# Pooled attention with a feed-forward block: the last 128 keys' scores on all 128 rows, transposes behind the feed-forward's unit, heads in alternation

## The chip, the cores and the metric

The kernel runs on one core of one Trainium2 chip. A time is device microseconds (us) of one execution; three executions of the kernel before took 892.95, 895.72 and 897.29 us, median 895.72.

The engines are named as in the profile: PE is TensorE's matrix multiplications, PEld its loading of the stationary operand, DVE is VectorE, ACT ScalarE, POOL GpSimd, SP SyncE, which issues nearly all DMAs here. PSUM is the accumulator memory, eight banks of 512 fp32 columns on 128 partitions.

## The reference

```python
# q, k, v: (4 batches, 8 heads, 1152 positions, 64) fp32
q_pool = q.reshape(B, H, S // 2, 2, D).mean(axis=3)           # 576 pooled queries
scores = scale * np.matmul(q_pool, k.transpose(0, 1, 3, 2))   # 576 x 1152 a head
scores = scores - np.max(scores, axis=-1, keepdims=True)
attn = np.exp(scores); attn = attn / (np.sum(attn, axis=-1, keepdims=True) + 1e-09)
x = np.matmul(attn, v)        # heads side by side: (4, 576, 512)
xn = (x - mean) / np.sqrt(var + 1e-06) * g_ln
out = x + np.maximum(xn @ w_ch1, 0.0) @ w_ch2                 # 512 -> 2048 -> 512
```

## The kernel before

**Precision.** Most products are made of fp16 halves: an fp32 operand is scaled by a power of two and split into `hi` (fp16 of it) and `lo` (fp16 of the rest), and a product is three matmuls, hi by hi, hi by lo and lo by hi. ACT writes `hi` from PSUM, DVE writes `lo` (`split_from`, L267).

**Steps.** The 16 pairs of heads (4 batches of 4 pairs, `p`) have 9 steps each (`j`), 144 in all (`i = 9p + j`). A step is 128 pooled queries of one head against all 1152 keys; step `j == 4` has the last 64 queries of both heads. Before the change `j` 0 to 3 are the first head's four full chunks and 5 to 8 the second head's. A step's chain is: scores on PE (`emit_s`, L320), row maximum on DVE (L350), exponential on ACT (L364), fp16 halves on ACT (L378) and on DVE or, in every third step, POOL (L387, L385), a DMA transpose issued by SP (L390), and four steps after the scores attention times values on PE (`emit_pv`, L433). The first batch (steps 0 to 35) takes another way: PE transposes the fp32 exponentials itself (L397) and L421 multiplies in fp32, while DVE, ACT and POOL also prepare the feed-forward's weights.

**Scores.** Head dimension is 64, so a score matmul contracts 64 rows. Keys and queries lie twice on the partitions, 0 to 63 and 64 to 127. Keys 0 to 511 are taken from the upper 64 rows and keys 512 to 1023 from the lower 64, in turns (`wide`, L332), so that two matmuls of 512 columns run side by side in two halves of the array. The last 128 keys (`kt[..., 512:640]`) follow as three matmuls on rows 0 to 63 alone. PSUM holds two score slots of three banks; step `i` issues the scores of step `i + 1`, which wait until the exponential of step `i - 1` has left its slot.

**Preparation.** Six pieces of the next pair are transposed on PE, one a step (`PREPS`, L304, `a_prep`, L897): `prep_k` 0 and 1 (a head's first 1024 keys, fp32, 128 rows), `prep_k` 2 (the last 128 keys of both heads), `prep_q` 0 to 2 (six transposes of 64 rows each).

**Feed-forward.** When a block of 128 output rows has all 8 heads (`evacuated`, L879) it is queued for its norm (DVE, POOL, four PE transposes at L532 two steps later). With two blocks normed, `units_of` queues "units": `l1`, 24 matmuls of 256 columns (L569), and `l2`, 12 of 512 (L600; two units a block and weight half). From step 36 on at most one unit is issued a step (`some_units`, L902), after the last step two. One batch has 32 units, 36 steps pass a batch. Units, transposes and norms share PSUM banks 6 and 7 (`bank`, L501), and their evacuations wait in `evacs` for `flush` in the next step.

**Order.** Each engine runs in the order in which the Python program issues. `step` (L924) sets it: the row maximum, the scores of `i + 1`, `flush`, exponential, halves, norm, then on PE attention times values (`a_piece`), preparation (`a_prep`), unit (`some_units`).

Of the kernel before, what the change touches and what calls it, by code (L numbers as in the profile page):

```python
# [24 lines left out]
def tile_pooled_attention_moe(  # L25
# [33 lines left out]
    NORM_AT = (3, 4, 5, 6, 7)  # L59
# [52 lines left out]
    def load(p, which, eng):  # L112
        b, hp = divmod(p, HP)
        h = 2 * hp
        src = k if which == "k" else v
        r = raw_p.tile([128, 2, C, D], FP32, tag=which + "r", name=which + "r")
        eng.dma_start(out=r, in_=src[b, h:h + 2].rearrange("h (p c) d -> p h c d", c=C))
        raws[p, which] = r
# [26 lines left out]
    def kt_of(p):  # L145
        st = state(p)
        if "kt" not in st:
            st["kt"] = tr_p.tile([128, 2, 2, 640], FP16, tag="kt", name="kt")
        return st["kt"]
# [20 lines left out]
    def bound(p, which, o=0, n=128, junk=None):  # L170
# [4 lines left out]
        else:  # L175
            src = raws[p, which][o:o + n].rearrange("p a b d -> p (a b d)")
            if junk is None:
                junk = kt_of(p)[o:o + n].rearrange("p a h n -> p (a h n)")[:, 0:S]
        m = "kqv".index(which)
# [5 lines left out]
    def all_max(src, n, then):  # L185
# [8 lines left out]
        def one():  # L194
# [82 lines left out]
    def prep_k(p, u):  # L277
# [8 lines left out]
        for h in range(2):  # L286
            nc.tensor.transpose(ps[0:64, 128 * h:128 * h + 128], kr[:, h, C - 1], ident)
        x = ps[0:64, 0:256].rearrange("p (h n) -> p h n", h=2)
        return split_from((p, "k", 2), x, s[0:64, 0:1], kt[0:64, 0, :, 512:640], kt[0:64, 1, :, 512:640])

    def prep_q(p, u):
# [4 lines left out]
        ps = bank()  # L296
        for m in range(6):
            nc.tensor.transpose(
                ps[:, 64 * m:64 * m + 64], qr[:, 6 * u + m], ident[o:o + 64, o:o + 64]
# [4 lines left out]
    PREPS = ((prep_k, 0), (prep_k, 2), (prep_q, 0), (prep_q, 1), (prep_k, 1), (prep_q, 2))  # L304
# [15 lines left out]
    def emit_s(i):  # L320
# [3 lines left out]
        if j == 4:  # L324
            parts = [(h, h * C * 64 + 512, 64, 64 * h) for h in range(2)]
        else:
            h = 0 if j < 4 else 1
            parts = [(h, h * C * 64 + 128 * (j if h == 0 else j - 5), 128, 0)]
# [3 lines left out]
        wide = ((64, 0, 512, 0), (0, 512, 512, 0))  # L332
        for here in (wide, ((0, 1024, 128, 512),)):
            for a, r, c0, n, k0 in [(a, *x) for a in range(3) for x in here]:
                ka, qa = ((0, 0), (1, 0), (0, 1))[a]
                for h, q0, w, o in parts:
                    nc.tensor.matmul(  # L337
                        out=sp[o:o + w, c0:c0 + n],
                        lhsT=qt[r:r + 64, qa, q0:q0 + w],
                        rhs=kt[r:r + 64, ka, h, k0:k0 + n],  # L340
                        start=(a == 0),
                        stop=(a == 2),
                    )
        steps[i] = {"s": sp[:, 0:S]}
# [60 lines left out]
    def emit_pv(i, ps=None):  # L405
# [9 lines left out]
        else:  # L415
            parts = [(0 if j < 4 else 1, 0, 128, ps[:, 0:65])]
# [40 lines left out]
    def evac_pv(i, ps):  # L457
# [10 lines left out]
        else:  # L468
# [4 lines left out]
            h = 0 if j < 4 else 1  # L473
            o, n, m = 0, 128, 1
            x = xb[b][:, j - 5 * h, 128 * hp + 64 * h:128 * hp + 64 * h + 64]
# [77 lines left out]
    def half_of(w, xn, xs, stores, free=()):  # L553
# [36 lines left out]
        def l2(t, f0):  # L590
            if t == 0 and f0 == 4:
                flush()
            if f0 == 0:
# [4 lines left out]
            for f in range(f0, f0 + 4):  # L598
                for ha, wa in ((0, 0), (0, 1), (1, 0)):
                    nc.tensor.matmul(  # L600
                        out=ps,
                        lhsT=hv[0][:, ha, f, t * 128:t * 128 + 128],
                        rhs=wsl[:, 8 * w + 4 + f // 2, wa, (f % 2) * DM:(f % 2) * DM + DM],
                        start=(f == 0 and ha == 0 and wa == 0),
# [472 lines left out]
```

## Time and profile before

| | |
|---|---|
| median of three executions | 895.72 us |
| profiled execution, its own time | 892.43 us |
| its span, first to last instruction | 890.6 us |
| PE busy | 837.2 us, 94% |
| DVE busy | 611.8 us, 69% |
| ACT busy | 568.4 us, 64% |
| POOL busy | 346.6 us, 39% |
| mean granted TensorE clock | 0.98 of full speed |

Busy time of an engine is the time in which at least one of its instructions runs; PE's matmuls overlap, so a group of n matmuls is busy for less than n times the mean duration of one. How often PE can start a matmul is read from the start times of two groups in the timeline. The granted clock has two levels, 1.2 and 2.4 GHz, and a share between stands for a stretch with both.

### The profile page before, as it was taken

The numbers are of one execution on the slowest core, as the hardware profiler recorded it, in microseconds if no ns is written. First come the engines' busy times: TensorE is split into PE (matmuls) and PEld (weight loads), VectorE is DVE, ScalarE is ACT, GpSimd is POOL, SyncE is SP. The second block draws the span as 40 slices with busy tenths as digits, with TensorE's granted clock in tenths as the row PEclk, the third lists the DMA queues.
The fourth block names the chain that finished last, engine by engine and source line by source line (L and its number), as shares of the span: only waits on it lengthen the run. The fifth ranks groups of instructions, "written<-read, shape, count | busy, mean of one in ns | idle before, by whom it ended". The sixth has DMA issues, their size and how long they took to land.

```text
span 890.6 us, 22107 instructions
## 1 busy us (share of the span) xinstructions
PE 837.2 (94%) x9430; PEld 608.2 (68%) x9430; DVE 611.8 (69%) x1094; ACT 568.4 (64%) x851; POOL 346.6 (39%) x316
## 2 busy tenths in 40 slices
PE   8898979899799999996999999998999999999997
PEld 6787768677566676754758576676667576776664
DVE  3586988888787777778777777787777777532211
ACT  4888788788677777776677777676767666211110
POOL 3010543543988844336435243535543422300000
PEclk9999999999899999997999999999999999999999
DMA  4554154403498779997896979895979778310001
GB/s 130 196 157 164 50 194 126 172 1 96 92 179 168 141 150 183 180 169 137 154 193 114 203 141 188 127 186 107 222 121 175 129 129 143 57 25 13 13 13 24
DMA packets 271667, 114.95 MB, mean 129 GB/s; under 512 B 254928, under 2 KB 254928, under 8 KB 271568
## 3 DMA queue, kind: packets, MB, share of 16 engines
q1 hardware_dynamic: 271216, 112.65, 61.4%
q8 instruction: 74, 1.21, 0.6%
q10 hardware_dynamic: 352, 0.88, 0.4%
q14 instruction: 25, 0.20, 0.1%
HBM read 45.09 MB, written 4.72 MB: 56 GB/s over the span
## 4 chain that ended last, share of the span: by engine, by line
PE 54%; DVE 25%; ACT 10%; DMA 5%; issue 3%; POOL 2%; SPq 1%; ACTq 0%; POOLq 0%; DVEq 0%
PE psum L569 15%; PE psum L600 15%; DVE mx L350 7%; PE psum L337 7%; PE psum L433 7%; DVE hl L387 4%; PE psum L421 4%; DVE stage L107 3%; ACT pe L364 3%; PE psum L397 2%; DVE ht L583 2%; DVE wsl L107 2%; DVE kt L270 2%; DMA qr<-in_q_dram 2%; DMA kr<-in_k_dram 1%
## 5 line engine op out<-in xcount | busy, mean ns | idle before, releaser
L350 DVE TENSOR_REDUCE mx<-psum 128x1 f32<-128x1152 f32 x144 | 194.2, 1349 | 27.1 <-PE psum L433 18.9
L364 ACT ACTIVATE pe<-psum,nb,sc 128x1152 f32<-128x1152 f32 x144 | 188.9, 1312 | 32.0 <-DVE nb L355 23.6
L600 PE MATMUL psum<-wsl,ht 128*128 128x512 f16 x864 | 196.0, 379 | 0.2 <-DVE ht L583 0.2
L569 PEld LDWEIGHTS <-wsl 128*128 128x128 f16 x1920 | 170.9, 98 | 22.7 <-issue 2.7
L569 PE MATMUL psum<-xn,wsl 128*128 128x256 f16 x1536 | 177.3, 274 | 1.9 <-DVE xn L539 1.0
L337 PE MATMUL psum<-kt,qt 64*128 64x512 f16 (+3 forms) x1440 | 151.8, 332 | 24.7 <-ACT xb L488 13.9
L337 PEld LDWEIGHTS <-qt 64*128 64x128 f16 (+1 forms) x1440 | 70.9, 98 | 116.0 <-issue 66.4
L600 PEld LDWEIGHTS <-ht 128*128 128x128 f16 x864 | 81.8, 98 | 90.0 <-issue 0.4
L378 ACT ACTIVATE hl<-pe 128x1152 f16<-128x1152 f32 x108 | 125.7, 1163 | 5.0 <-DMA pt<-hl 1.6
L433 PE MATMUL psum<-vt,pt 128*128 128x65 f16 (+1 forms) x3240 | 119.8, 195 | 0.0
L433 PEld LDWEIGHTS <-pt 128*128 128x128 f16 (+1 forms) x3240 | 108.1, 101 | 9.4 <-issue 0.6
L488 ACT ACTIVATE xb<-psum,r 128x64 f32<-128x64 f32 x128 | 39.7, 311 | 109.4 <-DVE r L484 100.1
L244 POOL TENSOR_SCALAR pe<-pe 128x1152 f32<-128x1152 f32 x36 | 41.9, 1164 | 164.0 <-ACT hl L378 153.7
L387 DVE SCALAR_TENSOR_TENSOR hl<-pe,hl 128x1152 f16<-128x1152 f32 x72 | 104.3, 1448 | 0.0
L582 ACT ACTIVATE ht<-psum 128x512 f16<-128x512 f32 x72 | 42.7, 594 | 90.6 <-PE psum L569 90.2
L583 DVE SCALAR_TENSOR_TENSOR ht<-psum,ht 128x512 f16<-128x512 f32 x72 | 49.6, 690 | 66.2 <-ACT ht L582 65.4
L385 POOL TENSOR_TENSOR hl<-pe,hl 128x1152 f16<-128x1152 f32 x36 | 86.4, 2400 | 3.0
L421 PE MATMUL psum<-pt,vt 128*65 128x128 f32 (+1 forms) x720 | 81.6, 271 | 0.0
L421 PEld LDWEIGHTS psum<-pt,vt 128*65 128x65 f32 x720 | 75.8, 144 | 0.2 <-issue 0.2
L270 DVE SCALAR_TENSOR_TENSOR qt<-psum,s,qt 128x384 f16<-128x384 f32 x48 | 29.6, 616 | 46.9 <-ACT qt L273 46.9
L270 DVE SCALAR_TENSOR_TENSOR kt<-psum,s,kt 128x512 f16<-128x512 f32 (+1 forms) x48 | 31.5, 658 | 39.1 <-ACT kt L273 39.1
L403 ACT COPY pt<-psum 128x512 f32<-128x512 f32 x72 | 44.9, 639 | 10.8 <-PE psum L397 5.5
(112 smaller groups left out, 925.6 us busy)
## 6 DMA issues: line engine op xcount, KB each, us to landing
stage<-in_moe_w_ch_dram SPq DMA_DIRECT2D x32, 512.0 KB, 5.5
kr<-in_k_dram SPq DMA_DIRECT2D x16, 576.0 KB, 4.7
qr<-in_q_dram SPq DMA_DIRECT2D x31, 288.0 KB, 6.2
vr<-in_v_dram SPq DMA_DIRECT2D x15, 576.0 KB, 4.9
out_dram<-xb SPq DMA_DIRECT2D x32, 128.0 KB, 2.4
pt<-hl SPq DMA_TRANSPOSE x108, 5.0
vr<-in_v_dram ACTq DMA_DIRECT2D x1, 576.0 KB, 6.5
out_dram<-xh SPq DMA_DIRECT2D x4, 128.0 KB, 3.5
```

Of the source, the lines that this page charges most:

```text
L270: nc.vector.scalar_tensor_tensor(lo, ps, s, hi, op0=ALU.mult, op1=ALU.subtract)
L337: nc.tensor.matmul(out=sp[o:o + w, c0:c0 + n], lhsT=qt[r:r + 64, qa, q0:q0 + w], rhs=kt[r:r + 64, ka, h, k0:k0 + n], start=(a == 0), stop= ...
L350: nc.vector.tensor_reduce(mx, st["s"], axis=AX.X, op=ALU.max)
L364: nc.scalar.activation(out=st["pe"], in_=st["s"], func=ACTF.Exp, scale=pair[i // C]["sc"][:, 0:1], bias=st["nb"],)
L378: nc.scalar.activation(out=hl[:, 0], in_=st["pe"], func=ACTF.Copy, scale=2.0 ** 15)
L385: nc.gpsimd.tensor_tensor(hl[:, 1], st["pe"], hl[:, 0], op=ALU.subtract)
L387: nc.vector.scalar_tensor_tensor(hl[:, 1], st["pe"], 2.0 ** 15, hl[:, 0], op0=ALU.mult, op1=ALU.subtract)
L421: nc.tensor.matmul(out=ps[0:65, q0:q0 + w], lhsT=vt[:, h, c], rhs=pt[:, 128 * u + q0:128 * u + q0 + w], start=(u == 0), stop=(u == C - 1),)
L433: nc.tensor.matmul(out=dst[:, 0:n], lhsT=lhsT, rhs=rhs, start=(u == 0 and lhsT is hi and n == 65), stop=(u == C - 1 and lhsT is lo), skip_ ...
L569: nc.tensor.matmul(out=ps[:, o:o + n], lhsT=wsl[:, 8 * w + cc, wa, f * 128:f * 128 + 128], rhs=xn[:, xa * KD + cc, 0:n], start=(m == 0), s ...
L583: lambda: nc.vector.scalar_tensor_tensor(lo, pv, 0.0, hi, op0=ALU.max, op1=ALU.subtract),
L600: nc.tensor.matmul(out=ps, lhsT=hv[0][:, ha, f, t * 128:t * 128 + 128], rhs=wsl[:, 8 * w + 4 + f // 2, wa, (f % 2) * DM:(f % 2) * DM + DM] ...
```

## The change

1. The last 128 keys of a head are stored as `k8`, `hi` on rows 0 to 63 and `lo` on rows 64 to 127 (`prep_k` 2 transposes the chunk beside a copy of itself, which a second, small DMA puts next to it). Two matmuls on all 128 rows, query `hi` and query `lo` against `k8`, take the place of three on 64 rows. The product lo by lo is thereby added.
2. `some_units` stands ahead of `a_prep` in a step, and in `PREPS` `prep_k` 1 stands ahead of `prep_q` 1.
3. In the last two pairs of each batch (`p % 4` of 2 and 3) the heads alternate (`PLACES`), so that an output block has all its heads earlier and the four blocks of a batch come further apart.
4. In the first batch's units the second block's `l2` is three units of 8 matmuls and not two of 12 (`fine`).
5. In `all_max` one small DVE operation reads PSUM (`max(ps, mx) * ident`) in place of SBUF.

```diff
+    PLACES = [[(h, t) for h in range(2) for t in range(4)], [(h, t) for t in range(4) for h in range(2)]]
+    for x in PLACES:
+        x.insert(C // 2, None)
...
+        x = src[b, h:h + 2].rearrange("h (p c) d -> p h c d", c=C)
+        if which == "k":
+            r = raw_p.tile([128, 2, C + 1, D], FP32, tag="kr", name="kr")
+            eng.dma_start(out=r[:, :, 0:C], in_=x)
+            eng.dma_start(out=r[:, :, C], in_=x[:, :, C - 1])
...
-                nc.vector.tensor_scalar(dg[0:n, 0:n], ident[0:n, 0:n], mx[0:n], None, op0=ALU.mult)
+                nc.vector.scalar_tensor_tensor(
+                    dg[0:n, 0:n], ps[0:n, 0:n], mx[0:n], ident[0:n, 0:n], op0=ALU.max, op1=ALU.mult
+                )
...
         for h in range(2):
-            nc.tensor.transpose(ps[0:64, 128 * h:128 * h + 128], kr[:, h, C - 1], ident)
-        x = ps[0:64, 0:256].rearrange("p (h n) -> p h n", h=2)
-        return split_from((p, "k", 2), x, s[0:64, 0:1], kt[0:64, 0, :, 512:640], kt[0:64, 1, :, 512:640])
+            x = kr[:, h, C - 1:C + 1].rearrange("p c d -> p (c d)")
+            nc.tensor.transpose(ps[:, 128 * h:128 * h + 128], x, ident)
+        x = ps[:, 0:256].rearrange("p (h n) -> p h n", h=2)
+        k8 = pair[p]["k8"]
+
+        def low():
+            nc.vector.scalar_tensor_tensor(
+                k8[64:128], x[64:128], s[64:128, 0:1], k8[64:128], op0=ALU.mult, op1=ALU.subtract
+            )
+            have.add((p, "k", 2))
+
+        return (lambda: nc.scalar.activation(out=k8, in_=x, func=ACTF.Copy, scale=s[:, 0:1]), low)
...
-    PREPS = ((prep_k, 0), (prep_k, 2), (prep_q, 0), (prep_q, 1), (prep_k, 1), (prep_q, 2))
+    PREPS = ((prep_k, 0), (prep_k, 2), (prep_q, 0), (prep_k, 1), (prep_q, 1), (prep_q, 2))
...
-            parts = [(h, h * C * 64 + 128 * (j if h == 0 else j - 5), 128, 0)]
+            parts = [(PLACES[p % HP // 2][j][0], 128 * j, 128, 0)]
...
+        for qa in range(2):
+            for h, q0, w, o in parts:
+                nc.tensor.matmul(
+                    out=sp[o:o + w, 1024:1152],
+                    lhsT=qt[:, qa, q0:q0 + w], rhs=pair[p]["k8"][:, h],
+                    start=(qa == 0), stop=(qa == 1),
+                )
...
-            (2 * w + 1, 2 + f0 // 2, lambda t=t, f0=f0: l2(t, f0))
-            for t in range(len(xs)) for f0 in (0, 4)
+            (2 * w + 1, (m1 + 5) // 6, lambda t=t, m0=m0, m1=m1: l2(t, m0, m1))
+            for t in range(len(xs))
+            for m0, m1 in (((0, 8), (8, 16), (16, 24)) if t and fine else ((0, 12), (12, 24)))
...
-            pre(i0 + (4, 5, 6, 6, 7, 8)[n] + late, lambda fn=fn, p=p, u=u: preps.append((fn, p, u)))
+            pre(i0 + 4 + n + late, lambda fn=fn, p=p, u=u: preps.append((fn, p, u)))
...
-        key = ("h", b // 2) if j == 4 else (b, j if j < 4 else j - 5)
+        key = ("h", b // 2) if j == 4 else (b, PLACES[p % HP // 2][j][1])
...
                 a_piece(i)
+            some_units(i)
             a_prep()
-            some_units(i)
```

What stands on PE around a step's query transposes, in a step of the second half. Before (`pt` is the transposed attention, `qr` the raw queries, `ht` the feed-forward's hidden layer):

```order
L433 LDWEIGHTS pt
L433 MATMUL psum<-vt,pt 128x65
L298 MATMUL psum<-ident,qr 128x64 x6
L600 LDWEIGHTS ht
L600 MATMUL psum<-wsl,ht 128x512
```

The unit stands between the transposes and the next scores. In the changed kernel, the same place to the end of the next scores (L632 is `l2`, L325 the transposes, L362 and L370 the scores, L464 attention times values; `qt` are the transposed queries):

```order
L632 MATMUL psum<-wsl,ht 128x512
L325 MATMUL psum<-ident,qr 128x64 x6
L362 LDWEIGHTS qt
L362 MATMUL psum<-kt,qt 128x512
...
L370 LDWEIGHTS qt
L370 MATMUL psum<-kt,qt 128x128
L370 LDWEIGHTS qt
L370 MATMUL psum<-kt,qt 128x128
L464 LDWEIGHTS pt
```

The transposes moved behind the unit and stand right before the scores, as they do in 28 of the 33 steps with query transposes from step 42 on (in the other five a norm's transposes stand between); before, a unit follows them in all 33. The last 128 keys are two matmuls; before they are three, with `L337` rows of the same look.

ACT around steps 74 to 76, where one batch's units have ended and the next batch's begin. Before (`pe` is the exponential, `hl` its half, `xb` an output block, `xn` a normed block, `ht` an `l1` unit's evacuation):

```order
L364 ACTIVATE pe<-psum,nb,sc 128x1152
L378 ACTIVATE hl<-pe 128x1152
L180 ACTIVATE kt,acc<-vr 128x1152
L488 ACTIVATE xb<-psum,r 128x64
L364 ACTIVATE pe<-psum,nb,sc 128x1152
L378 ACTIVATE hl<-pe 128x1152
L488 ACTIVATE xb<-psum,r 128x64
L538 CAST xn<-psum 128x4x128
L364 ACTIVATE pe<-psum,nb,sc 128x1152
L378 ACTIVATE hl<-pe 128x1152
L488 ACTIVATE xb<-psum,r 128x64
L273 ACTIVATE kt<-psum,s 128x512
```

The same stretch in the changed kernel:

```order
L395 ACTIVATE pe<-psum,nb,sc 128x1152
L409 ACTIVATE hl<-pe 128x1152
L191 ACTIVATE kt,acc<-vr 128x1152
L519 ACTIVATE xb<-psum,r 128x64
L395 ACTIVATE pe<-psum,nb,sc 128x1152
L409 ACTIVATE hl<-pe 128x1152
L519 ACTIVATE xb<-psum,r 128x64
L613 ACTIVATE ht<-psum 128x512
L395 ACTIVATE pe<-psum,nb,sc 128x1152
L409 ACTIVATE hl<-pe 128x1152
L519 ACTIVATE xb<-psum,r 128x64
L613 ACTIVATE ht<-psum 128x512
```

The rows run from the exponential of step 74 to the evacuations behind that of step 76. An `l1` unit's evacuation (`ht`) stands behind the exponentials of steps 75 and 76; before, the first one stands behind that of step 78. Counted over all steps from 36 on, PE has no unit in steps 36 to 40 and 73 to 77 in the kernel before, and in steps 36, 37 and 74 in the changed one; the first batch's units are 32 before and 36 now. On POOL, two norms stand between the first weight piece (L244 `wsl`) of step 36 and the low half (L385) of step 38 before, and one now.

## Rows read from the trace of the kernel before

**Rows 1.** Page, part 1: busy us, share, instructions of each engine.
```profile
PE 837.2 (94%) x9430; PEld 608.2 (68%) x9430; DVE 611.8 (69%) x1094; ACT 568.4 (64%) x851; POOL 346.6 (39%) x316
```

**Rows 2.** Windows: five stretches, busy us (instructions) of each engine, clock, DMA.
```profile
core 0: us, PE busy (x) PEld busy (x) DVE busy (x) ACT busy (x) POOL busy (x), PEclk, DMA share, GB/s
207.00:225.00 18.00, 15.11 (x130) 11.55 (x128) 15.91 (x34) 15.87 (x23) 9.35 (x17) 0.91 0.54 132
225.00:239.00 14.00, 9.75 (x104) 7.36 (x100) 11.76 (x21) 6.96 (x11) 13.47 (x13) 0.76 0.52 98
246.00:394.00 148.00, 145.31 (x1795) 99.31 (x1792) 112.16 (x201) 105.80 (x142) 92.05 (x65) 1.00 0.89 165
401.00:426.00 25.00, 17.46 (x215) 12.18 (x213) 20.48 (x45) 16.32 (x23) 18.12 (x26) 0.73 0.80 143
753.00:891.00 138.00, 132.88 (x1142) 92.78 (x1140) 40.11 (x72) 21.36 (x39) 7.97 (x17) 1.00 0.14 27
```

**Rows 3.** Timeline of stalls: start us, us, engine, work, [idle before <-releaser].
```profile
230.62 1.31 ACT L364 ACTIVATE pe<-psum,nb,sc 128x1152 f32<-128x1152 f32 x1 [5.00 <-POOL hl L385]
231.99 1.78 PE L337 MATMUL psum<-kt,qt 64*128 64x512 f16 x9 [3.67 <-ACT pe L364]
...
404.98 1.81 PE L337 MATMUL psum<-kt,qt 64*64 64x512 f16 x18 [2.82 <-ACT pe L364]
...
419.81 0.63 PE L287 MATMUL psum<-ident,kr 128*64 128x128 f32 x2 [3.92 <-DVE kt L270]
```

**Rows 4.** Matmul groups by shape: busy us, mean ns of one, idle before.
```profile
L337 PE MATMUL psum<-kt,qt 64*128 64x512 f16 x768 | 110.2, 385 | 6.3 <-ACT pe L364 3.7 <-ACT pt L403 2.1 <-DVE qt L270 0.3
L337 PE MATMUL psum<-kt,qt 64*128 64x128 f16 x384 | 42.6, 218 | 13.6 <-ACT xb L488 12.0 <-ACT xh L488 1.6
L569 PE MATMUL psum<-xh,wsl 128*128 128x128 f16 x384 | 22.6, 219 | 0.7 <-DVE xn L539 0.7
L337 PE MATMUL psum<-kt,qt 64*64 64x128 f16 x96 | 5.6, 222 | 2.0 <-ACT xb L488 1.9
```

**Rows 5.** Timeline of TensorE, query transposes ahead of a unit.
```profile
567.42 0.99 PE L433 MATMUL psum<-vt,pt 128*128 128x65 f16 x27
568.34 0.58 PE L298 MATMUL psum<-ident,qr 64*128 64x64 f32 x6
568.86 2.76 PE L600 MATMUL psum<-wsl,ht 128*128 128x512 f16 x12
571.55 0.99 PE L337 MATMUL psum<-kt,qt 64*128 64x512 f16 x9
572.47 1.90 PE L433 MATMUL psum<-vt,pt 128*64 128x65 f16 x54
```

**Rows 6.** Timeline of TensorE, a step with key transposes.
```profile
552.06 0.99 PE L433 MATMUL psum<-vt,pt 128*128 128x65 f16 x27
552.88 0.63 PE L284 MATMUL psum<-ident,kr 128*128 128x128 f32 x4
553.35 2.78 PE L569 MATMUL psum<-xn,wsl 128*128 128x256 f16 x24
```

**Rows 7.** Timeline of TensorE, query transposes ahead of scores, two places.
```profile
56.73 0.46 PE L298 MATMUL psum<-ident,qr 64*128 64x64 f32 x4
...
57.90 0.42 PE L700 MATMUL psum<-g,stage 128*128 128x1 bf16 x8
...
98.46 0.40 PE L298 MATMUL psum<-ident,qr 64*128 64x64 f32 x3
...
99.80 0.43 PE L700 MATMUL psum<-ones,stage 128*128 128x1 bf16 x8
```

**Rows 8.** Page, parts 5 and 6: L433 matmuls, key loads, DMA transposes.
```profile
L433 PE MATMUL psum<-vt,pt 128*128 128x65 f16 (+1 forms) x3240 | 119.8, 195 | 0.0
kr<-in_k_dram SPq DMA_DIRECT2D x16, 576.0 KB, 4.7
pt<-hl SPq DMA_TRANSPOSE x108, 5.0
```

More of the change, by code (lines that the diff above doesn't have):

```diff
@@ L115, in load @@
         src = k if which == "k" else v
-        r = raw_p.tile([128, 2, C, D], FP32, tag=which + "r", name=which + "r")
-        eng.dma_start(out=r, in_=src[b, h:h + 2].rearrange("h (p c) d -> p h c d", c=C))
+        x = src[b, h:h + 2].rearrange("h (p c) d -> p h c d", c=C)
[3 more added lines that the diff above has]
+            eng.dma_start(out=r[:, :, C], in_=x[:, :, C - 1])
+        else:
+            r = raw_p.tile([128, 2, C, D], FP32, tag="vr", name="vr")
+            eng.dma_start(out=r, in_=x)
         raws[p, which] = r
@@ L324, in emit_s @@
         if j == 4:
-            parts = [(h, h * C * 64 + 512, 64, 64 * h) for h in range(2)]
+            parts = [(h, 128 * j + 64 * h, 64, 64 * h) for h in range(2)]
         else:
-            h = 0 if j < 4 else 1
-            parts = [(h, h * C * 64 + 128 * (j if h == 0 else j - 5), 128, 0)]
+            parts = [(PLACES[p % HP // 2][j][0], 128 * j, 128, 0)]
         for h, q0, w, o in parts:
@@ L331, in emit_s @@
             assert need <= have, (i, need - have)
[L332 to L335, printed above, removed]
+        for a in range(3):
+            ka, qa = ((0, 0), (1, 0), (0, 1))[a]
+            for r, c0 in ((64, 0), (0, 512)):
                 for h, q0, w, o in parts:
                     nc.tensor.matmul(
[L338 to L342, printed above, removed]
-                    )
+                        out=sp[o:o + w, c0:c0 + 512],
+                        lhsT=qt[r:r + 64, qa, q0:q0 + w], rhs=kt[r:r + 64, ka, h],
+                        start=(a == 0), stop=(a == 2),
+                    )
+        for qa in range(2):
[5 more added lines that the diff above has]
+                )
         steps[i] = {"s": sp[:, 0:S]}
@@ L597, in l2 @@
             ps = acc[t]
[L598 to L604, printed above, removed]
-                        stop=(f == 7 and ha == 1),
-                    )
-            if f0 == 0:
+            for m in range(m0, m1):
+                f = m // 3
+                ha, wa = ((0, 0), (0, 1), (1, 0))[m % 3]
+                nc.tensor.matmul(
+                    out=ps,
+                    lhsT=hv[0][:, ha, f, t * 128:t * 128 + 128],
+                    rhs=wsl[:, 8 * w + 4 + f // 2, wa, (f % 2) * DM:(f % 2) * DM + DM],
+                    start=(m == 0), stop=(m == 23),
+                )
+            if m1 < 24:
                 return ()
@@ L827, in half @@
                 w, keep["xn", u], [xb[b][:, u], xb[b][:, u + 1]],
-                [[(64 * s, rows(b, 2 * x + s)) for s in range(2)] for x in (u, u + 1)],
+                [[(64 * s, rows(b, 2 * x + s)) for s in range(2)] for x in (u, u + 1)], b == 0,
             )
```

33 lines of the change are left out of this document (19 added, 14 removed).

## The prediction

> **What bounds the kernel now.** I read the page's busy times first: PE is busy for 837.2 of 890.6 us, DVE for 611.8 [rows 1]. An average hides stages, so the windows came next. In the long stretches of the second half PE is busy for 145.3 of 148 us at the full clock, and in the tail, where only feed-forward units are left, for 132.9 of 138, while DVE has 112.2 of 148 and 40 of 138 [rows 2]. There, what PE does sets the time: a microsecond less work on PE is a microsecond less. In two stretches it is not so. From 225 to 239 us, where the first batch's attention is done and its feed-forward has not begun, PE is busy for 9.75 of 14 us at a granted clock of 0.76; from 401 to 426, between the first batch's units and the second's, for 17.5 of 25 us at 0.73 [rows 2]. The timeline names the waits: PE stands 3.67 us for an exponential that itself stood 5.00 us for POOL, then 2.82 us for an exponential and 3.92 us for DVE's half of the keys [rows 3]. A clock of 0.76 means that part of the stretch ran at 1.2 GHz in place of 2.4; both low stretches begin with PE standing. Units are work without a deadline, so whatever PE loses here is not made up: the tail is as long as the units left over.
>
> So the change has two ways to gain, less PE work and fewer of these holes.
>
> **Narrow scores (the last 128 keys).** Three matmuls of 128 columns are busy for 42.6/128 = 0.333 us together, one lasts 0.218, so they start (0.333 - 0.218)/2 = 0.058 us apart [rows 4]. A matmul of 128 columns on all 128 rows costs 22.6/384 = 0.059 us in a stream [rows 4]. Three become two, so a step saves 0.058; 128 full steps give 7.4 us. The 16 steps of half chunks have three couples of 64-wide matmuls, busy 5.6/16 = 0.35 us [rows 4]; they become four matmuls, and I put them at nothing.
>
> The trace has no matmul on 128 rows behind one on 64 rows within the scores. It has the change between them elsewhere: from attention times values to query transposes (64 rows) takes 0.92 us, to key transposes (128 rows) 0.82 [rows 5, 6], so going from 128 to 64 rows costs 0.10. For the way back I take the same. A step's scores have one change at each end before and after; it moves from behind the narrow matmuls to ahead of them, at no cost. Bounds: if a second change is paid, the term is 128 x (0.058 - 0.10) = -5.4 us; if the change is hidden under the last wide matmul, 128 x (0.058 + 0.10) = +20. I take 7.4, the value of rows of the same shape.
>
> The Trainium skill ("TensorEngine Tiling (Array Packing)", Tiling Modes) says that changing the tiling mode drains the TensorE. The trace agrees that a change costs, but with 0.10 us. A wide matmul lasts 0.385 [rows 4] and the next starts 0.216 later (12 of 512 columns take 2.69 - 0.10 [rows 5]), so a full emptying behind it would cost 0.17. By that rule the term would be 7.4 - 128 x 0.07 = -1.6 us.
>
> The new product's preparation stays off PE's path: ACT and DVE take 256 columns as before, the transposes are as many. They hide behind PE's step of some 5 us (30 steps in the 148 us of the long window [rows 2]); DVE's spare time there is 36 of 148 us.
>
> **Query transposes behind the unit.** Before, a step with them goes from 567.42 to 572.47: attention times values with the change of rows 0.92, transposes with the change back 0.52, unit 2.69 with a change, scores 0.92 [rows 5]. In the changed order attention times values go to the unit without a change (0.82, [rows 6]), the unit to the transposes with one, and the transposes to the scores without. That last border is in the trace, in the first batch, where no units are: transposes and scores together take 57.90 - 56.73 = 1.17 us where the queries lie on the upper 64 partitions (odd pairs) and 99.80 - 98.46 = 1.34 on the lower (even pairs) [rows 7], against 0.52 + 0.92 = 1.44 apart. The first scores run beside the last transposes, in the other half of the array. With the 0.10 at the front, odd pairs save 0.37 a piece and even ones 0.20. Of the 33 steps concerned, 28 get the scores directly behind (11 odd, 17 even, counted in the order); five have a norm between and keep three changes. Sum: 11 x 0.37 + 17 x 0.20 = 7.5 us. Key transposes use 128 rows like the units on both sides, so their move is worth nothing.
>
> **The holes.** The order has no unit in five steps at each of the two places before, and in two and one now. At 401 to 426, full-speed work is at most 17.46 x 0.73 = 12.7 us, so 12.3 are lost [rows 2]; one step of five keeps a fifth, 9.8 come back. At 225 to 239, 14 - 9.75 x 0.76 = 6.6 are lost. The exponential's wait behind POOL has one norm less in its queue, and units are there three steps earlier; I let 1.1 remain and count 5.5. The loss of 18 - 15.11 x 0.91 = 4.3 at 207 to 225 lies in steps 36 to 38 and is kept. Bounds for both together: nothing, if the hole only moves, and 19 us, if it closes. The third batch's border shows no such hole and counts nothing. The split into units of 8 adds no matmul; it serves to fill four more steps and is priced in this term.
>
> **What is added.** Each pair's key load gets a second DMA of 64 KB, a ninth of a load that lands in 4.7 us [rows 8]; SP issues it behind that load and ahead of DMA transposes. Cost between 0.5 (a ninth) and 4.7 us a pair. Transposes land in 5.0 us and are read three steps, some 15 us, after their issue, and attention times values have an idle time of 0.0 [rows 8], so I cost it at nothing; without that cover it would be 0.5 to 4.7 us on each of 11 pairs. The small DVE operation in `all_max` is one for one.
>
> **Sum.** 7.4 + 7.5 + 9.8 + 5.5 = 30.2 us. The profiled execution took 892.43 us, which gives 862.2; the median of the runs is 3.3 above that execution, so I forecast 865.5, written as 865.
>
> **Rivals.**
> 1. *DVE or ACT becomes the bound in the refilled steps.* DVE is busy for 20.5 of 25 us and 11.8 of 14 in the two holes [rows 2], with the norms' work among it; units add evacuations there. Against it: the norms come further apart, and PE's lack of work made the steps stand on a chain, not on DVE's throughput. If half of the holes' 15.3 us stays, the time is 873.
> 2. *The narrow matmuls pay a change on both sides*, -5.4 in place of 7.4: 878. For it: nothing in the trace shows this border. Against it: one end of the scores loses its change. Milder, *the array empties behind the wide matmuls*, 0.17 in place of 0.10 a step, -1.6 in place of 7.4: 874; the borders in [rows 5, 6] speak against it. This is what the Trainium skill's rule above would give.
> 3. *The narrow border is hidden* under the wide matmuls, or waits for PSUM banks shrink too: up to 12 us better, 853.
> 4. *Slower: the DMA queue falls behind.* The DMA share is 0.89 over 148 us [rows 2], and a faster PE raises it to about 0.92. If the extra transfer costs a whole load (4.7 us) with no cover, each of 11 pairs makes PE stand for it: 52 us, 865 + 52 = 917. It decides once transposes land later than three steps after issue, that is 15 in place of 5 us [rows 8]; idle time of 0.0 there speaks against it. The Trainium skill ("DMA: Bandwidth & Descriptors", Specifications) asks for 512 B a transfer for full rate, and the new rows have 256; by that the small DMA runs slower than its size says, which no row here shows.
>
> **How the numbers follow.** Forecast (857 to 871) 0.60; rival 1, 0.15; rival 2, 0.06, and the emptying 0.03; rival 3, 0.08; rival 4, 0.03; and 0.05 for holes that stay as they are with a dear narrow border (7.5 - 5.4 = 2 us gained, 893). The range of 853 to 878 takes in rivals 1 to 3 up to their prices and leaves out the last two and the tails. About 0.5%, 4.5 us, is what a measurement of this kernel tells from no change: faster by more 0.92, within 0.05, slower 0.03.
>
> **What would show it.** Narrow scores: from the first score matmul to what follows 0.86 us in place of 0.92; 0.96 is rival 2. Query steps: transposes and scores together 1.1 to 1.3 us. Holes: no wait over 2 us on PE between 225 and 426, granted clock over 0.9 in both stretches, or else rival 1. DMA: L433's successor still without idle time. The tail behind the last step must be shorter by about what the holes gave. I am wrong if PE's busy time falls by less than 10 us, or if waits on DVE or ACT take over what it gives up.

## The result and the profile after

The changed kernel takes 883.98 us (median of 4 runs, 880.98 to 886.67), the kernel before beside it 896.5 (892.95 to 898.92): ratio 0.987, 95% interval 0.984 to 0.990. It is 12.5 us faster, where 30 were forecast; 884 lies outside the range of 853 to 878. The profiled execution of after took 883.46 us, with a span of 881.7.

The page's busy times answer to [rows 1], and four windows to [rows 2]; the last is shorter because the run is. Lines of after: units L600 and L632 (before L569, L600), scores L362 and, narrow, L370 (L337), attention times values L464 (L433), query transposes L325 (L298), `all_max` L207 (L196), ACT's bounds L191 (L180).

```profile
PE 823.7 (93%) x9270; PEld 587.6 (67%) x9270; DVE 614.7 (70%) x1092; ACT 570.7 (65%) x851; POOL 349.0 (40%) x318
```

```profile
225.00:239.00 14.00, 11.34 (x129) 8.56 (x127) 11.55 (x18) 7.20 (x9) 8.69 (x10) 0.88 0.42 80
246.00:394.00 148.00, 137.40 (x1699) 90.61 (x1700) 115.01 (x200) 103.90 (x137) 88.93 (x66) 0.98 0.86 161
401.00:426.00 25.00, 21.68 (x288) 15.62 (x283) 21.05 (x42) 19.06 (x26) 10.87 (x16) 1.00 0.86 156
753.00:882.00 129.00, 124.01 (x1063) 85.09 (x1061) 35.95 (x65) 19.99 (x36) 7.83 (x15) 0.99 0.14 29
```

PE's work fell by 13.5 us, the time by less. The two holes did fill: work at full speed rose from 12.7 to 21.7 us at 401 to 426 and from 7.4 to 10.0 at 225 to 239 (busy by clock), 11.6 of the 15.3 forecast. Behind the last attention times values the run lasts 110.0 us in place of 118.5. But the steps up to there end when they did, at 771.7 us (before: 772.1): what is gained is the feed-forward units that they took in, and nothing shows of less work in the steps themselves. The stretch between the holes, where PE had been busy for 145.3 of 148 us at the full clock, now stands for 10.6 us at 0.98.

PE's waits in the steps from 240 to 755 us, first before, then after (engine, line, releaser: us in total, times, longest):

```profile
PE psum L287 <- DVE kt L270: 3.9, 1, 3.9
PE psum L337 <- ACT pe L364: 2.8, 1, 2.8
PE psum L196 <- ACT kt L180: 2.8, 3, 1.1
```

```profile
PE psum L207 <- ACT kt L191: 7.8, 6, 2.1
PE psum L600 <- DVE xb L645: 4.3, 3, 2.0
PE psum L632 <- DVE ht L614: 3.4, 4, 0.9
PE psum L563 <- DVE qt L283: 2.8, 2, 1.4
```

The single long waits of 2.8 and 3.9 us are gone. The largest is now that of `all_max`'s transposes for ACT's bounds, mostly in every second pair. Three waits of some 2 us, one for xb and two for the bounds, and a window of 4 us behind each show what such a wait is followed by:

```profile
268.12 4.24 PE L600 MATMUL psum<-xn,wsl 128*128 128x256 f16 x24 [1.97 <-DVE xb L645]
...
364.03 0.27 PE L207 MATMUL psum<-ident,acc 128*3 128x128 f32 x1 [2.12 <-ACT kt L191]
...
548.79 0.27 PE L207 MATMUL psum<-ident,acc 128*3 128x128 f32 x1 [1.73 <-ACT kt L191]
```

```profile
269.00:273.00 4.00, 4.00 (x30) 2.37 (x27) 2.78 (x5) 3.97 (x6) 0.76 (x1) 0.57 1.08 254
364.50:368.50 4.00, 4.00 (x39) 3.07 (x36) 2.85 (x7) 2.85 (x4) 0.51 (x2) 0.57 1.12 156
549.00:553.00 4.00, 4.00 (x44) 3.23 (x42) 2.94 (x7) 2.92 (x4) 1.28 (x2) 0.57 1.37 176
```

PE is busy throughout, at a granted clock of 0.57, that is at 1.2 GHz for 3.4 of the 4 us: (1 - 0.57) x 4 = 1.7 us lost each. Before, windows of 4 us at 269, 364 and 547 had 1.00.

### The profile page after: what moved, and what is told of

It is laid out like the page before. It is cut to its first block, busy times and chain, and to the rows that moved or that the text cites. A ratio compares the mean times of both kernels' runs of the same rounds, so it can differ in the third digit from the quotient of the medians.

```text
span 881.7 us, 21840 instructions
## 1 busy us (share of the span) xinstructions
PE 823.7 (93%) x9270; PEld 587.6 (67%) x9270; DVE 614.7 (70%) x1092; ACT 570.7 (65%) x851; POOL 349.0 (40%) x318
## 4 chain that ended last, share of the span: by engine, by line
PE 51%; DVE 26%; ACT 13%; DMA 4%; issue 3%; POOL 1%; SPq 1%; ACTq 0%; POOLq 0%; DVEq 0%
PE psum L632 15%; PE psum L600 14%; DVE mx L381 7%; PE psum L464 6%; DVE hl L418 5%; PE psum L362 4%; PE psum L452 4%; ACT pe L395 3%; DVE stage L109 3%; DVE ht L614 2%; PE psum L428 2%; ACT ht L613 2%; DVE wsl L109 2%; PE psum L370 2%; DVE kt L283 1%
## 5 line engine op out<-in xcount | busy, mean ns | idle before, releaser
L632 PE MATMUL psum<-wsl,ht 128*128 128x512 f16 x864 | 196.6, 379 | 3.9 <-DVE ht L614 3.4
L600 PEld LDWEIGHTS <-wsl 128*128 128x128 f16 x1920 | 171.9, 99 | 29.5 <-issue 9.2
L600 PE MATMUL psum<-xn,wsl 128*128 128x256 f16 x1536 | 181.7, 277 | 8.4 <-DVE xb L645 4.3
L632 PEld LDWEIGHTS <-ht 128*128 128x128 f16 x864 | 80.8, 98 | 92.3 <-issue 4.5
L362 PE MATMUL psum<-kt,qt 64*128 64x512 f16 (+1 forms) x960 | 127.4, 381 | 1.7 <-ACT pe L395 0.9
L464 PE MATMUL psum<-vt,pt 128*128 128x65 f16 (+1 forms) x3240 | 117.6, 194 | 0.0
L464 PEld LDWEIGHTS <-pt 128*128 128x128 f16 (+1 forms) x3240 | 109.5, 100 | 2.5 <-DMA pt<-hl 0.4
L418 DVE SCALAR_TENSOR_TENSOR hl<-pe,hl 128x1152 f16<-128x1152 f32 x72 | 109.3, 1518 | 0.0
L362 PEld LDWEIGHTS <-qt 64*128 64x128 f16 (+1 forms) x960 | 39.8, 97 | 39.7 <-issue 22.3
L370 PEld LDWEIGHTS <-qt 128*128 128x128 f16 (+1 forms) x320 | 17.8, 99 | 72.5 <-issue 72.0
L370 PE MATMUL psum<-kt,qt 128*128 128x128 f16 (+1 forms) x320 | 41.4, 226 | 12.1 <-ACT xb L519 10.6
```

Source lines behind the costliest of these rows:

```text
L362: nc.tensor.matmul(out=sp[o:o + w, c0:c0 + 512], lhsT=qt[r:r + 64, qa, q0:q0 + w], rhs=kt[r:r + 64, ka, h], start=(a == 0), stop=(a == 2),)
L370: nc.tensor.matmul(out=sp[o:o + w, 1024:1152], lhsT=qt[:, qa, q0:q0 + w], rhs=pair[p]["k8"][:, h], start=(qa == 0), stop=(qa == 1),)
L418: nc.vector.scalar_tensor_tensor(hl[:, 1], st["pe"], 2.0 ** 15, hl[:, 0], op0=ALU.mult, op1=ALU.subtract)
L464: nc.tensor.matmul(out=dst[:, 0:n], lhsT=lhsT, rhs=rhs, start=(u == 0 and lhsT is hi and n == 65), stop=(u == C - 1 and lhsT is lo), skip_ ...
L600: nc.tensor.matmul(out=ps[:, o:o + n], lhsT=wsl[:, 8 * w + cc, wa, f * 128:f * 128 + 128], rhs=xn[:, xa * KD + cc, 0:n], start=(m == 0), s ...
L632: nc.tensor.matmul(out=ps, lhsT=hv[0][:, ha, f, t * 128:t * 128 + 128], rhs=wsl[:, 8 * w + 4 + f // 2, wa, (f % 2) * DM:(f % 2) * DM + DM] ...
```

## The experiments

Each is measured in 5 rounds against the kernel before, whose median was 894.9 to 895.9; an interval is some 2.5 us to either side, so a difference of two rows under some 3.5 us tells little. "Bounds" is PE's waits for L191 or its like from 240 to 755 us.

| run | us | ratio, 95% interval | bounds, us |
|---|---|---|---|
| undo_narrow | 883.63 | 0.987 (0.984 to 0.990) | 9.4 |
| undo_order | 887.36 | 0.991 (0.988 to 0.994) | 7.3 |
| undo_heads | 891.22 | 0.995 (0.992 to 0.998) | 7.9 |
| undo_thirds | 881.82 | 0.985 (0.982 to 0.988) | 6.8 |
| narrow_alone | 894.19 | 0.999 (0.996 to 1.001) | 5.5 |
| order_alone | 892.90 | 0.997 (0.994 to 0.999) | 7.3 |
| heads_alone | 886.41 | 0.989 (0.985 to 0.992) | 5.3 |
| one_narrow | 886.54 | 0.989 (0.985 to 0.994) | 13.2 |
| early_k | 892.66 | 0.997 (0.995 to 0.999) | 11.7 |
| late_max | 912.50 | 1.019 (1.015 to 1.023) | 0 |
| late_max_halves | 909.99 | 1.017 (1.014 to 1.020) | 0 |
| early_q | 875.46 | 0.978 (0.974 to 0.981) | 1.9 |
| early_q_load | 874.05 | 0.976 (0.973 to 0.979) | 4.1 |
| before_early_q | 896.17 | 1.001 (0.999 to 1.003) | 0 |
| early_q_one_narrow | 873.13 | 0.975 (0.972 to 0.977) | 2.2 |
| early_q_undo_order | 879.05 | 0.981 (0.979 to 0.984) | 1.4 |
| early_q_undo_narrow | 874.53 | 0.978 (0.976 to 0.981) | 1.4 |
| early_q_undo_heads | 885.20 | 0.989 (0.987 to 0.991) | 0 |

**What each part is worth.** Four kernels undo one part of after; three do one part alone on before. Narrow (undo_narrow and, the other way round, narrow_alone):

```diff
-        for qa in range(2):
...
-                    lhsT=qt[:, qa, q0:q0 + w], rhs=pair[p]["k8"][:, h],
...
+        for here in (wide, ((0, 1024, 128, 512),)):
+            for a, r, c0, n, k0 in [(a, *x) for a in range(3) for x in here]:
...
+                        rhs=kt[r:r + 64, ka, h, k0:k0 + n],
```

> The changed kernel with the scores' last 128 keys done as before (three narrow matmuls on 64 rows per full step, no second key transfer); the other two parts of the change stay. The theory: the narrow scores are worth 0.044 us in a full step (0.920 to 0.876 us in the traces) and cost about 0.07 us in a half-chunk step, so 108 steps of feed-forward-era work give about 4 us; this kernel is then at 888 us. The forecast's own sum (7.4 us) would put it at 891. Rival: the second key transfer delays the bound and the all_max transposes (3.1 us of waits on L207 between 255 and 400 us) as much as the narrow scores save, and the time stays at 884 or falls below.

> The kernel before with the new narrow scores alone (and the second key transfer they need). Undoing them in the changed kernel cost nothing (883.6 against 884.0 us). Theory A: each full step really gets 0.04 us shorter, and in the changed kernel the shorter steps run into waits of another engine; on the kernel before, whose steps 46 to 66 show 1.6 us of TensorE waits between 255 and 400 us, the saving shows: 892 us, 4 less. Theory B: the new operands cost as much as they save wherever they stand (half-chunk steps 0.07 us dearer, mode changes, the second transfer): 896. The forecast's own term would give 889.

Nothing undone, 1.7 us alone, where the interval takes in no change: theory B, nearly. The rival with the second transfer falls too: without it the waits for the bounds are no smaller (9.4). Where the time of the shorter product goes stands in the timeline of TensorE. A plain step and a step whose next work has fewer columns, in after:

```profile
559.28 0.82 PE L362 MATMUL psum<-kt,qt 64*128 64x512 f16 x6
560.03 0.28 PE L370 MATMUL psum<-kt,qt 128*128 128x128 f16 x2
560.15 0.98 PE L464 MATMUL psum<-vt,pt 128*128 128x65 f16 x27
...
574.03 0.82 PE L362 MATMUL psum<-kt,qt 64*128 64x512 f16 x6
574.79 0.28 PE L370 MATMUL psum<-kt,qt 128*128 128x128 f16 x2
575.00 1.90 PE L464 MATMUL psum<-vt,pt 128*64 128x65 f16 x54
```

From the first score to what follows it is 0.87 in the one and 0.97 in the other, against 0.92 in [rows 5]: the change moves ahead of the narrow matmuls as forecast, but where the successor has another shape (64 columns, or the 3 rows of a matmul of `all_max`) it is paid behind them as well. And a step with queries of an odd pair, with the old product (undo_narrow: transposes L307, scores L345, attention times values L441) and the new (after):

```profile
259.83 0.46 PE L307 MATMUL psum<-ident,qr 64*128 64x64 f32 x4
260.08 0.39 PE L345 MATMUL psum<-kt,qt 64*128 64x512 f16 x1
260.13 0.28 PE L307 MATMUL psum<-ident,qr 64*128 64x64 f32 x2
260.26 0.81 PE L345 MATMUL psum<-kt,qt 64*128 64x512 f16 x8
261.00 0.99 PE L441 MATMUL psum<-vt,pt 128*128 128x65 f16 x27
```

```profile
260.37 0.46 PE L325 MATMUL psum<-ident,qr 64*128 64x64 f32 x4
260.62 0.39 PE L362 MATMUL psum<-kt,qt 64*128 64x512 f16 x1
260.67 0.28 PE L325 MATMUL psum<-ident,qr 64*128 64x64 f32 x2
260.80 0.81 PE L362 MATMUL psum<-kt,qt 64*128 64x512 f16 x5
261.54 0.29 PE L370 MATMUL psum<-kt,qt 128*128 128x128 f16 x2
261.66 0.98 PE L464 MATMUL psum<-vt,pt 128*128 128x65 f16 x27
```

1.17 us with the old product, 1.29 with the new, in 15 such steps; in the 13 of even pairs 1.33 and 1.29. From 240 us on the query transposes and scores of all steps, standing left out, take 105.6 us with the old product and 107.0 with the new (0.3 of it from steps at the lower clock): nothing is saved.

Order (the same two lines, swapped):

```diff
-            some_units(i)
             a_prep()
+            some_units(i)
```

> The changed kernel with the key and query transposes ahead of the feed-forward's unit again. The theory: the order brings 7 us of fewer mode changes but also the new waits of TensorE on banks and on ht (L600, L632 and L563: 9.6 us between 240 and 400 us in the trace of the changed kernel, 1.4 before), so that the two cancel and the time is 884 with 3 us to either side, with those waits under 4 us. Rival 1 (VectorE and ScalarE bind the refilled steps, whatever the order): the mode changes come back and the waits stay, 891 us. Rival 2 (the transposes' place is worth more than the forecast): over 893.

> The kernel before with the key and query transposes behind the feed-forward's unit, and nothing else. Undone in the changed kernel it cost 3.4 us of the forecast 7.5. Theory A (the mode changes are saved as forecast, and bank waits in the refilled steps take a part back): on the kernel before, which has few such waits, 6 to 7 us, 889 to 890 us. Theory B (the order itself brings waits: a unit right behind a second-layer unit asks for the bank that is still being emptied): 893, with waits of the first layer's matmuls on the emptying of xb of over 2 us between 255 and 400 us.

3.4 us undone, just past the theory's range, with the waits it named at 3.6 us as it said, and 3.0 alone, theory B's time. The first of the two is hardly clear of the noise (the intervals of undo_order and after overlap). Work is saved, if not quite the 7.5 us forecast: alone, PE is busy for 489.8 of the 515 us from 240 on, before for 497.2, with nine matmuls fewer in the window; over the whole run, with as many matmuls, its busy time falls by 5.3 us (837.2 to 831.9).

```profile
240.00:755.00 515.00, 497.23 (x6220) 343.00 (x6218) 386.32 (x705) 363.51 (x485) 247.89 (x210) 0.99 0.85 157
```

```profile
240.00:755.00 515.00, 489.75 (x6211) 341.73 (x6210) 384.01 (x705) 365.72 (x487) 249.34 (x212) 0.98 0.84 157
```

So the saved work became standing time. But theory B's mechanism fell: waits for xb did not take it (none of the first layer's alone). More than half of it is waits for the bounds, which rose from 2.8 to 7.3 with no narrow scores and no second transfer.

Heads and thirds (heads_alone is the reverse, on before):

```diff
-    PLACES = [[(h, t) for h in range(2) for t in range(4)], [(h, t) for t in range(4) for h in range(2)]]
+    PLACES = [[(h, t) for h in range(2) for t in range(4)], [(h, t) for h in range(2) for t in range(4)]]
...
-                [[(64 * s, rows(b, 2 * x + s)) for s in range(2)] for x in (u, u + 1)], b == 0,
+                [[(64 * s, rows(b, 2 * x + s)) for s in range(2)] for x in (u, u + 1)], False,
```

> The changed kernel with a pair's heads one after the other in every pair and the second layer in halves everywhere, as before; the narrow scores and the new order stay. The theory: the refilled holes gave 8.7 and 3.1 us, and the new waits and clock drops in the steps that were stretched over the first batch's units took some 11 to 14 us, so that this part of the change was worth nothing: 883 us with 3 us to either side, the new waits gone and the two holes back. Rival (the waits come from the order, not from the heads): the holes come back and the waits stay, 893 us or more.

> The kernel before with alternating heads, thirds in the first batch's second layer, and the transposes of the second key head one place earlier (they must be); old narrow scores, transposes ahead of the unit. The forecast's terms for the two holes would give 881 us (15.3 less). The theory that most of the holes' gain is waited away in the steps that now carry the units: 7 us, 889, with waits of TensorE of over 8 us between 255 and 400 us (1.6 before). Rival (the waits need the shorter steps that the other two parts make): 883 or less, with waits under 5 us.

> The changed kernel with the first batch's second-layer units in halves of 12 matmuls everywhere, not in thirds of 8. The theory that a bank held over three steps causes the new waits (4.3 us on L600 behind xb): 880 us, these waits under 1 us. The theory that the thirds only fill the second hole (16 units spread over more steps): the stretch runs dry some four steps earlier and the time is 886 to 888. If neither: 884 within 1.5.

7.2 us undone, 9.5 alone, of 15.3. heads_alone lies between its theories' times, with the waits of the first (8.1 us between 255 and 400). The waits for the bounds do not need the alternation: they stay at 7.9 us when it is undone, and the time is nearer to the rival's. In undo_thirds only the second edit is made. The waits on L600 for xb fall from 4.3 to 0.4 us, as its first theory said, but others come (3.4 us for VectorE's qt, 3.1 for an exponential), and the time (881.8) cannot be told from that of after; the 886 to 888 of its second theory falls.

**What a microsecond of TensorE work is worth.**

```diff
-        for qa in range(2):
+        for qa in range(1):
```

> The changed kernel with one of the two narrow score matmuls of each row group left out (the product of the queries' low half with the last 128 keys is not computed). It takes 0.066 us of TensorE work out of each of 128 full steps, 90 of them behind the first batch. It measures what a microsecond of TensorE work taken out is worth. Theory A (TensorE sets the time behind the first batch, other engines within it): 90 x 0.066 = 6 us, 878. Theory B (in the first batch TensorE waits for ScalarE anyway, and behind it the shorter steps run into other engines' turns): a third of that or less, 882 or more. The forecast's way of counting (all 128 steps): 8.4 us, 875.6.

Nothing, theory B: 886.5. PE's work falls again, from 823.7 to 817.4 us, and the waits for the bounds grow from 7.8 to 13.2.

```profile
PE 817.4 (92%) x9110; PEld 583.0 (66%) x9110; DVE 614.6 (69%) x1092; ACT 569.9 (64%) x851; POOL 347.7 (39%) x318
```

**What the bounds wait for.** The queue of SyncE in after, ahead of the wait at 268 to 274 us:

```profile
249.99 2.67 SPq L421 DMA_TRANSPOSE pt<-hl  x1
252.71 2.50 SPq L137 DMA_DIRECT2D qr<-in_q_dram  x4
255.38 6.23 SPq L421 DMA_TRANSPOSE pt<-hl  x1
261.71 0.52 SPq L121 DMA_DIRECT2D kr<-in_k_dram  x1
262.28 0.46 SPq L122 DMA_DIRECT2D kr<-in_k_dram  x1
```

```profile
268.30 1.16 ACT L191 ACTIVATE kt<-kr 128x1152 f16<-128x1152 f32 x1 [3.51 <-DMA kr<-in_k_dram]
...
274.50 0.27 PE L207 MATMUL psum<-ident,acc 128*3 128x128 f32 x1 [0.98 <-ACT kt L191]
```

In every second pair four query loads stand ahead of a transposing DMA. Its entry then lasts 4.8 to 6.2 us in the five places of after (5.25 to 5.93 in before), where the median of all others is 2.75. What stands behind it is late. The key load is: ACT stands 3.51 us for it here, at the head of its own queue, and 5.7 us in five places together (0.9 in before). So are transposing DMAs, which still read the tiles that ACT writes next: 4.7 us in five places (1.6 in before). Ahead of the longest wait for the bounds, 2.12 us at 364.03, ACT stood for such a tile and hardly for the key:

```profile
355.64 1.17 ACT L409 ACTIVATE hl<-pe 128x1152 f16<-128x1152 f32 x1 [2.64 <-DMA pt<-hl]
356.96 1.16 ACT L191 ACTIVATE kt<-kr 128x1152 f16<-128x1152 f32 x1 [0.15 <-DMA kr<-in_k_dram]
```

Three edits test the chain from the query load to `all_max`. The first, early_k:

```diff
-        at(max(i0 - 1, 0), load, p, "k", nc.sync)
+        at(max(i0 - (1 if on_pe(i0) else 2), 0), load, p, "k", nc.sync)
```

> The changed kernel with the key load of a pair one step earlier on SyncE's queue, ahead of the query loads and of the transposing DMA behind them, from the fifth pair on. Theory A: in every second pair the key load stands behind four query loads and a transposing DMA that takes 5.6 to 6.8 us beside them, lands too late for ScalarE's bound (ScalarE idle 3.5 us at 268 us, 5.3 in four such places), and TensorE's all_max transposes and what is behind ScalarE wait with it: without it the waits on L207 (7.8 us over the span) go under 3 us and the time is 878. Theory B: VectorE and GpSimd hold these steps anyway (the 3.42 us subtraction beside the pooled-query add at 262 us): 884, the waits only change their name.

Wrong on both sides: 8.7 us slower than after. Keys and queries now stand on the queue together and the transposes behind them land late (the entry behind the query loads lasts 6.1 to 7.1 us). ACT stands 19.8 us for the tiles that they still read (4.7 in after), and attention times values for the first time (5.9):

```profile
L409 ACT ACTIVATE hl<-pe 128x1152 f16<-128x1152 f32 x108 | 125.6, 1163 | 23.1 <-DMA pt<-hl 19.8
...
L464 PE MATMUL psum<-vt,pt 128*128 128x65 f16 (+1 forms) x3240 | 117.8, 194 | 5.9 <-DMA pt<-hl 5.9
```

The second, late_max (and late_max_halves, with the edit of undo_thirds):

```diff
-        elif reds:
-            evacs.append(reds.popleft()())
...
             some_units(i)
+            if reds:
+                evacs.append(reds.popleft()())
             a_prep()
```

> The changed kernel with the all_max transposes of a pair put behind the step's feed-forward unit on TensorE, not between the scores and attention times values. In every trace so far these transposes wait for ScalarE's bounds (7.8 us between 255 and 760 us in the changed kernel, 2.9 before), and a lower granted clock follows the longest of these waits. Theory A (the saved TensorE work runs into this one wait, and the unit behind it could have been done meanwhile): these waits go under 2 us, and 4 to 6 us come back, 878 to 880. Theory B (what binds the short steps is ScalarE's and VectorE's turn itself, not one wait): the time moves to other waits, 884 within 2.

> The same with the first batch's second-layer units in halves everywhere. Halves alone came to 881.8 against 884.0. If the two are independent: 876 under theory A of the run before, 882 under B.

The waits for the bounds went, but the edit made a dearer one. `all_max` writes in the bank of the next step's scores, so that VectorE's maximum of that step now stands for it behind the unit:

```profile
327.30 1.36 DVE L381 TENSOR_REDUCE mx<-psum 128x1 f32<-128x1152 f32 x1 [2.80 <-PE psum L207]
```

It tells nothing between its theories.

The third, early_q, of which early_q_load makes only the first changed line, and before_early_q all on the kernel before:

```diff
+            e = 0 if on_pe(i0 - 2) else 2
-            at(i0 - 2, load_q, p, (nc.sync,))
-            pre(i0 + 1, pool_q, p, nc.gpsimd)
-            at(i0 + 1, dup_q, p, nc.gpsimd)
-            at(i0 + 2, bound, p, "q")
+            at(i0 - 2 - e, load_q, p, (nc.sync,))
+            pre(i0 + 1 - e, pool_q, p, nc.gpsimd)
+            at(i0 + 1 - e, dup_q, p, nc.gpsimd)
+            at(i0 + 2 - e, bound, p, "q")
```

> The changed kernel with the query loads, the pooled add, its copy and the queries' bound two steps earlier, from the seventh pair on, so that every second pair no longer has the key load behind the query loads on SyncE and three bounds in two steps on ScalarE. Theory (ScalarE's burst of bounds and the late key load make the all_max wait): waits on L207 under 3 us, ScalarE's idle time before the key bound under 1 us (5.3 now), time 879. Rival (moving a load only moves what it collides with, as the key load one step earlier did, 892.7): 884 or more, with waits on the transposing DMA's tiles.

> The changed kernel with only the query loads two steps earlier; the pooled add, its copy and the queries' bound stay where they were. If the loads' place on SyncE's queue (ahead of a transposing DMA and the key load) is what made the bounds late: 877 or less. If it is ScalarE's three bounds in two steps or the pooled add on GpSimd beside VectorE's subtraction: 882 to 884.

> The kernel before with the query loads and what follows them (pooled add, copy, bound) two steps earlier from the seventh pair on, as in the run that brought the changed kernel to 875.5. Theory (a chain from the query load to the all_max of every second pair has a length of its own; the old kernel's longer steps mostly covered it, with 2.9 us of waits on the all_max between 255 and 760 us, and the change's shorter steps do not, with 7.8): little to gain here, 0 to 3 us, 893 to 896. Rival (the early queries help any kernel alike, whatever the steps' length): 887.

Early queries bring 8.5 us to after (5 expected) and nothing to before; that was the theory, and its rival fell. On the kernel before the waits for the bounds go as well (2.8 to 0 us), but those of the query transposes for xb and kt grow from 2.0 to 5.1 us: there another wait was as near. early_q_load moves the load alone and brings as much, so the link is the loads' place on SyncE, not GpSimd's add or the three bounds on ScalarE. Its queue, its waits and its long windows:

```profile
243.13 2.81 SPq L137 DMA_DIRECT2D qr<-in_q_dram  x4
246.10 13.64 SPq L421 DMA_TRANSPOSE pt<-hl  x3
259.85 0.53 SPq L121 DMA_DIRECT2D kr<-in_k_dram  x1
260.43 0.47 SPq L122 DMA_DIRECT2D kr<-in_k_dram  x1
```

```profile
PE psum L207 <- ACT kt L191: 4.1, 5, 1.4
...
PE psum L600 <- DVE xb L645: 1.8, 2, 1.0
```

```profile
246.00:394.00 148.00, 138.55 (x1755) 91.78 (x1754) 115.59 (x206) 107.10 (x143) 95.32 (x73) 1.00 0.89 168
364.50:368.50 4.00, 4.00 (x57) 3.19 (x54) 3.24 (x4) 3.06 (x4) 0.00 (x0) 1.00 1.02 200
```

Three transposes now lie between query and key load, ACT never stands for the keys and 1.2 us for a tile, no wait from 240 us on reaches 2 us, and the clock of the long window is 1.00. Waits shorter by 3.7 us for the bounds and by 2.5 for xb, and three stretches of 1.7 at the lower clock, are 11.3 us, beside 9.9 gained. The waits for xb need not go for that: early_q keeps them (4.5 us) and gains nearly as much. At 874.05 us it beats both kernels. But 9.5 us of standing stay at 246 to 394, where before had 2.7.

**The parts without the chain** (each is early_q and one edit from above):

> The changed kernel with the early queries and with the second narrow score product left out (the queries' low half with the last 128 keys is not computed). Without the early queries leaving it out brought nothing (886.5 against 884.0). Theory (the chain of the queries was what turned saved TensorE work into waits): with the chain gone the 90 steps behind the first batch give 0.066 us each again, 6 us: 869 to 870. Rival (the other engines' turn binds the steps in general): 874 to 876.

> The changed kernel with the early queries, and the key and query transposes ahead of the unit again. In the traces the new order takes 7.4 us of TensorE work out of the steps between 240 and 755 us, as forecast, but it was worth 3.0 (alone) and 3.4 us (undone). Theory (the chain took the rest): with the chain gone it is worth 6 to 7.5, 882 to 883. Rival (its own waits for banks took the rest): 879.

> The changed kernel with the early queries and the old narrow scores (three narrow matmuls on 64 rows, no second key transfer). Counted by borders in the changed kernel's trace, from 240 us on: 69 full steps are 0.045 us shorter, 21 whose next work is on fewer columns or rows are 0.049 us longer, 11 half-chunk steps 0.065 us longer, 1.4 us in all, and the first batch's steps wait for ScalarE anyway. Theory (the borders count, the chain hid nothing of it): 876 to 877.5. Rival (without the chain the forecast's 7.4 us appear): 882 to 883.

> The changed kernel with the early queries, a pair's heads one after the other in every pair and halves everywhere. Without the early queries the alternation was worth 7.2 us (undone) and 9.5 (alone). Theory (the chain lay in the steps that the alternation fills, and took the rest of what the two holes gave): worth 11 to 13 now, 886.5 to 888.5. Rival (the units' own waits in those steps took it): 7 to 9 again, 882.5 to 884.5.

Against early_q's 875.46: a narrow product left out gives 2.3 us (6 expected; within the noise), the order is worth 3.6, the narrow scores nothing (-0.9), the heads 9.7. The first two times are the rivals' and not the theories': with the chain broken, work taken out of TensorE is still not worth its length, so something else holds the order's other 4 us. So the chain hid much of the whole but not much of each single part: undone one at a time they give 12.4 us, all together (896.2 to 875.5) 20.7. Of the 30.2 us forecast 9.5 are then still missing, not much more than the term of the narrow scores (7.4). Why the parts do not add was not settled; with one part gone another wait can take its place, as the waits for DVE's ht, qt and xb in after's list suggest.

## Why the prediction was wrong

- **The step that failed first** is the one behind the whole sum, "a microsecond less work on PE is a microsecond less". It was read from steps in which PE was busy for 98%, but an engine with no idle time may hide a chain that is just as long. The chain from query load to `all_max` fitted into the old steps (waits of 2.8 us) and not into the shorter ones. Breaking it gives 8.5 to 9.9 us back to after and nothing to before, about half of the 18 us that were missing. It was not all: with it broken, a narrow product and the order are still worth less than their work (2.3 of 6, 3.6 of 7.5 us), and what holds that back stays open.
- **Narrow scores, 7.4 us**, measured -0.3 undone and 1.7 alone: mis-sized. Three matmuls did become two, 0.066 apart. But the border was priced for one successor: 21 of 90 full steps pay it on both sides, 15 steps with queries of odd pairs lose 0.12 each, which the sum had already booked for the order; and in 12 of the first batch's 32 full steps PE stood for ScalarE in the middle of these very matmuls, 12.4 of the 13.6 us in [rows 4], so work taken out there was not on the path. Rival 2 was right for those 21 steps. The Trainium skill ("TensorEngine Tiling (Array Packing)", Tiling Modes) was the sounder warning: by its rule, that a change of tiling mode drains the engine, the term was -1.6. The runs agree that the term is gone, but by borders with other shapes, each about 0.1 us, not by an emptying of the array in each step (0.17 by the prediction's estimate).
- **Query transposes behind the unit, 7.5 us**, measured 3.0 alone: the work was about right (497.2 to 489.8 busy in the window, 5.3 us less over the run), its worth was not. The trace has 15 odd and 13 even steps, not 11 and 17, which at the term's own prices would be 8.2. Query steps are at 1.29 us, the upper end of the sign named, because of the narrow border.
- **The holes, 15.3 us**, measured 7.2 to 9.7: they filled (11.6 us by the windows), and the stretch between them gave a part back, 7.9 us more standing at 246 to 394. Rival 1 (873, "half of the holes' 15.3 us stays") comes nearest in kind: waits over 2 us remained between 225 and 426 (L600 for ht 2.67, L207 2.12) and the clock in the first hole was 0.88, both named as its signs.
- **Rival 4 had the place and not the mechanism.** It looked for the DMA queue's delay at attention times values, whose idle time of 0.0 [rows 8] did stay 0.0. The delay came out on the keys' side of the same queue. The second transfer it blamed costs nothing that can be seen.
- Right: PE's work fell by more than 10 us, and the tail is 8.5 us shorter, near what the holes gave. But waits on DVE and ACT took over what the steps gave up, the second sign of being wrong in the prediction's last sentence.

## What to carry to other kernels

Before counting saved work on a busy engine as time, measure the slack of the chains beside it: for each load, the time from its issue to its first reader, against the time of the steps between. A wait of 1 us that comes every second pair was the place where saved time stopped here, and a control on the old kernel (early queries: nothing) tells a new bound from an old one. Price a matmul of another shape by all its neighbours, not by one.

## What was not expected of the hardware

- On SyncE a transposing DMA behind four plain loads held the queue for 4.8 to 6.2 us in after; the median of the others is 2.75. What is issued behind it is late by the difference.
- In after three stands of TensorE of 1.7 to 2.1 us were each followed by 3.4 us at 1.2 GHz (0.57 over windows of 4 us) in the midst of busy steps, so that such a wait cost nearly twice its length.
- Two narrow matmuls on 128 rows start 0.066 us apart, and attention times values on 128 columns follows after 0.056, on 64 after 0.15.
